# Logits in two parts, v in two buffers, eight plain heads, and constants moved to ScalarE and GpSimd

## The chip, the cores and the metric

The kernel runs on one core of a Trainium2 chip. The metric is the device time of one execution in microseconds (us). The core's engines work side by side, each through its own queue in program order: TensorE (PE, with its weight loads as PEld), VectorE (DVE), ScalarE (ACT), GpSimd (POOL) and SyncE (SP), which only issues DMAs. An instruction waits for semaphores of the engines or DMAs that make its operands or free its output.

## What is computed

Attention over 4 batches of 12 heads, then a mixture of experts in which each token goes to one of 8.

```python
scores = scale * np.matmul(q, k.transpose(0, 1, 3, 2))       # (4, 12, 448, 64) each
scores = np.where(mask, -1000000000.0, scores)
attn = np.exp(scores - np.max(scores, axis=-1, keepdims=True))
attn = attn / (np.sum(attn, axis=-1, keepdims=True) + 1e-09)
x = np.matmul(attn, v)                                        # to (1792, 768)
logits = x @ w_gate + modality_bias[modality_id]              # (1792, 8)
e_idx = np.argmax(logits, axis=1)
gate_w = softmax(logits)[np.arange(N), e_idx]
for e in range(E):
    mask = e_idx == e
    h = np.maximum(x[mask] @ w1[e], 0.0)
    out[mask] = gate_w[mask, None] * (h @ w2[e])
```

## The kernel before

**Attention** is a software pipeline over 48 heads, `iteration(n)` for n = 0 to 47. Iteration n makes the scores of head n on PE (`st_scores`, L270) and their masked maximum on DVE (L280), the exponentials of head n-1 on ACT (`st_exp`, L290), the transposes of head n-2 on PE (`st_trans`, L302), its split into a high and a low part on ACT (`ph`, L320) and DVE (`pl`, L321), and the product with v of head n-3 (`st_pv`, L334 and L341, into the one PSUM bank `ot`). The output of head n-4 is put together on ACT (`hol`, L359) and DVE (`ut`, L365), which frees `ot`. Four heads are a group. `st_comb` (L394) multiplies a group's outputs, one of four row tiles in each iteration, by a matrix that holds the gate weights, into the one PSUM bank `x`, eight iterations behind the scores. `norm_l` (L412) and `norm_x` (L422) divide by the softmax sums; row tiles 0 to 2 do so on DVE straight from `x`, tile 3 is copied to `cxt` by ACT and divided on POOL. `rec`, the sums plus 1e-9 (`st_sums`, L372, on POOL), is inverted on DVE.

**Operands.** Each product is three float32r products of a high and a low part; six heads, 0 to 5, use plain float32 operands, four matmuls in place of eight shorter ones. The parts of q and k are made on POOL one pair of heads ahead of use (`split_qk`, L194 and L195, and `split_kl`, L200 and L202, four iterations ahead of the pair) and stacked by four DMAs on SP. The parts of v are made on POOL once in a group (`split_vh`, L242, and `split_vl`, L247, in iterations 2, 6, 10 and so on) from one buffer `vraw`.

**Routing.** `after_batch` sets the routing of a batch into the iterations that follow it, in lists of work that `run_todo` takes up at fixed places of an iteration. The gate logits of three groups lie in the tile `ltp`; `logits` (L454, DVE) sums them, `top`, `ties` and `choice` find the expert (DVE and POOL; `oh` is the choice as 0 and 1), and `places` counts with small matmuls into bank `x` (L476 to L482) at which place of its expert's list a token stands. ACT copies the counts to `pc` (L485). `scatter` writes tokens into four tables in DRAM by indirect DMAs (L501). After batch 1 `first_expert`, `first_slot`, `first_shift`, `first_base`, `first_tri` and `first_order` choose the expert that is computed first and set constants of the schedule, on DVE (L516 to L537) and POOL.

**Between attention and experts** the last heads and batch 3 are worked off, written out by hand: `w1_chunk` splits the first expert's weights on POOL, `pre_g1` does first-layer products (L751 to L753) of two blocks of tokens that are known already, six steps of 6 matmuls for each block. In between stand the choice and `places` of batch 3. `schedule_a` is one long chain of small DVE instructions (L580 to L589) on the final counts; `htl` (L782, DVE) is the low part of the hidden layer, which the second-layer products need. After it come the expert blocks, whose token lists are fetched from the tables (L720) and gathered (L732).

## Time and profile before

| | us |
|---|---|
| median of 3 runs | 498.74 (497.79 to 500.5) |
| the profiled execution | 498.88 |
| its span in the trace | 496.8 |
| PE busy | 470.7 (95%) |
| DVE, ACT, POOL busy | 290.3, 276.4, 245.8 |
| mean granted clock of TensorE | 0.987 |

The span runs from the first to the last instruction; some 2.1 us of the profiled time lie outside it. Attention takes the first 209 us or so, the experts the rest. The shares of busy time are means over both: in attention all four engines are busy nearly all the time, among the experts PE alone is. A waiting engine appears as a gap, with the instruction whose end released it. The granted clock is 1.00 at 2.4 GHz and 0.50 at 1.2 GHz.

### The profile page before, as it was taken

To read this page: it belongs to the slowest core of one execution; us is meant where nothing else is said; L and a number is where in the kernel's file an instruction comes from. 1 tells how busy PE (TensorE), PEld (TensorE's weight loads), DVE (VectorE), ACT (ScalarE), POOL (GpSimd) and SP (SyncE) were. 2 spreads that over 40 slices of the span, in tenths; PEclk is the share of its full clock that TensorE was granted. 3 is DMA by queue.
4 is the path that set the end of the run, shared out by engine and by line. 5 is a ranking of instruction groups with operands and counts; after the bars stand their busy time and mean duration, and the time that the engine had idled before them with its cause. 6 is when DMAs were issued, how large, how long until landed. Compare 5 with 4: busy or idle time off the path is not lost. (4 is left out here: it accounts for less than half of the span.)

```text
span 496.8 us, 10248 instructions
## 1 busy us (share of the span) xinstructions
PE 470.7 (95%) x3307; PEld 443.0 (89%) x3307; DVE 290.3 (58%) x858; ACT 276.4 (56%) x680; POOL 245.8 (49%) x332
## 2 busy tenths in 40 slices
PE   8999899999899979989999999999999999999990
PEld 6799899999798979869999999999999999889770
DVE  4899899999889988987422017431120120283490
ACT  5799899999788978326212116612220211383670
POOL 8999999999999999942301104102001001021131
PEclk9999999999899999989999999999999999999997
DMA  7797799998987889491596204853001001076200
GB/s 189 199 257 214 183 236 251 281 237 206 292 214 182 188 182 327 126 202 3 163 381 208 81 1 144 292 203 98 34 1 53 33 2 63 33 279 194 104 13 7
DMA packets 43816, 78.91 MB, mean 159 GB/s; under 512 B 15582, under 2 KB 27614, under 8 KB 43744
## 3 DMA queue, kind: packets, MB, share of 16 engines
q1 hardware_dynamic: 40624, 66.94, 49.2%
q0 software_dynamic: 3040, 11.03, 6.6%
q8 instruction: 28, 0.46, 0.5%
q14 instruction: 44, 0.36, 0.3%
q10 hardware_dynamic: 80, 0.11, 0.1%
HBM read 48.10 MB, written 11.89 MB: 121 GB/s over the span
## 5 line engine op out<-in xcount | busy, mean ns | idle before, releaser
L732 POOL DMA_INDIRECT xg<-xs,idg x18 | 21.0, 1164 | 156.6 <-DVEq L1336 80.8
L290 ACT ACTIVATE p<-p,nm 128x448 f32<-128x448 f32 x192 | 94.8, 498 | 2.5 <-DVE nm L280 2.5
L770 DVE SCALAR_TENSOR_TENSOR htl<-g,hth 128x256 fp32r<-128x256 f32 x40 | 16.7, 425 | 104.6 <-ACT hth L769 104.6
L751 PE MATMUL g<-xh,w1h 128*128 128x256 f32 x240 | 67.1, 280 | 0.4 <-DVE htl L770 0.4
L753 PE MATMUL g<-xh,w1l 128*128 128x256 f32 x240 | 67.3, 280 | 0.0
L752 PE MATMUL g<-xl,w1h 128*128 128x256 f32 x240 | 67.0, 279 | 0.0
L321 DVE TENSOR_TENSOR pl<-pt,ph 128x1024 fp32r<-128x1024 f32 x48 | 58.3, 1215 | 7.6 <-ACT ph L320 7.2
L302 PE MATMUL pt<-ident,p 128*128 128x128 f32 x480 | 60.2, 273 | 0.0
L302 PEld LDWEIGHTS pt<-ident,p 128*128 128x128 f32 x480 | 55.3, 141 | 1.1
L334 PE MATMUL ot<-ph,vhl 128*128 128x448 f32 x192 | 50.5, 303 | 5.9 <-DVE ut L365 5.9
L320 ACT ACTIVATE ph<-pt 128x1024 fp32r<-128x1024 f32 x48 | 49.1, 1023 | 7.4 <-PE pt L302 6.3
L769 ACT ACTIVATE hth<-g 128x256 fp32r<-128x256 f32 x40 | 15.1, 383 | 63.5 <-PE g L753 63.5
L751 PEld LDWEIGHTS g<-xh,w1h 128*128 128x128 f32 x240 | 44.9, 187 | 0.6 <-DVE htl L770 0.6
L811 POOL DMA_INDIRECT out_dram<-row,idg x14 | 16.2, 1157 | 59.1 <-ACTq L1320 33.5
L752 PEld LDWEIGHTS g<-xl,w1h 128*128 128x128 f32 x240 | 45.2, 188 | 0.0
L753 PEld LDWEIGHTS g<-xh,w1l 128*128 128x128 f32 x240 | 45.1, 188 | 0.0
L334 PEld LDWEIGHTS ot<-ph,vhl 128*128 128x128 f32 x192 | 33.2, 192 | 7.9 <-DVE ut L365 6.4
L280 DVE CUSTOM_DVE_ANT_0 p<-sa,mask 128x448 f32<-128x448 f32 x96 | 36.2, 412 | 5.2 <-PE sa L270 4.9
L290 ACT ACTIVATION_READ_ACCUMULATOR p<-p,nm 128x1 f32 x192 | 36.5, 190 | 0.0
L280 DVE CUSTOM_DVE_ANT_0 p<-sb,mask 128x192 f32<-128x192 f32 x96 | 36.3, 411 | 0.0
L341 PE MATMUL ot<-pl,vhl 128*64 128x64 f32 x192 | 35.1, 298 | 0.7 <-DVE pl L321 0.7
L359 ACT ACTIVATE hol<-ot 64x448 f32<-64x448 f32 x48 | 26.0, 542 | 13.3 <-PE ot L334 10.8
(365 smaller groups left out, 1307.6 us busy)
## 6 DMA issues: line engine op xcount, KB each, us to landing
st<-hl SPq DMA_DIRECT2D x56, 224.0 KB
raw<-in_moe_w_dram SPq DMA_DIRECT2D x24, 512.0 KB
raw<-in_qk_dram SPq DMA_DIRECT2D x21, 448.0 KB
raw<-in_moe_w_dram SPq DMA_DIRECT2D x20, 384.0 KB
vraw<-in_v_dram SPq DMA_DIRECT2D x12, 384.0 KB
xs<-row SPq DMA_DIRECT2D x9, 384.0 KB
w1h<-hl SPq DMA_DIRECT2D x14, 224.0 KB
w1l<-hl SPq DMA_DIRECT2D x14, 224.0 KB
```

What stands on the lines that cost most here:

```text
L280: V.tensor_tensor_reduce(out=z, in0=o, in1=m, scale=-scale, scalar=3.0e38, op0=ALU.add, op1=ALU.min, accum_out=nm[:n, i:i + 1],)
L290: A.activation(out=z, in_=z, func=AF.Exp, bias=nm[:n, i:i + 1], scale=-1.0, accum_out=sums[:n, b, i, h:h + 1],)
L302: nc.tensor.transpose(out=o, in_=a, identity=i)
L320: A.activation(out=ph, in_=t, func=AF.Copy)
L321: V.tensor_tensor(out=pl, in0=t, in1=ph.bitcast(F32), op=ALU.subtract)
L334: nc.tensor.matmul(o[:, q0:S], lhsT=t[:rows, kt, h].rearrange("p a d -> p (a d)"), rhs=ph[:rows, c0:c1], start=(n == 0), stop=(n == 1),)
L341: nc.tensor.matmul(o[0:D, q0:S], lhsT=t[:rows, kt, h, 0], rhs=pl[:rows, c0:c1], start=False, stop=False)
L359: A.activation(out=t, in_=ov[g][64:128, :S], func=AF.Copy)
L732: P.indirect_dma_start(out=xg[u][:n], out_offset=None, in_=xs[0:rows, :], in_offset=bass.IndirectOffsetOnAxis(ap=g[:n, 0:1], axis=0), boun ...
L751: nc.tensor.matmul(o, lhsT=ah, rhs=bh, start=first, stop=False)
L752: nc.tensor.matmul(o, lhsT=ah, rhs=bl, start=False, stop=False)
L753: nc.tensor.matmul(o, lhsT=al, rhs=bh, start=False, stop=last)
```

## The change

- Heads 6 and 7 are plain as well (`first_load(3)`): their splits on POOL and stacking DMAs fall away, and DVE fills two half tiles with zeros.
- v has a second buffer, `raw1[2]`. The high part is made in iterations 7, 11, 15 and so on, the low part an iteration later; the first group's low part is made on DVE.
- `st_sums` is an ACT instruction.
- `part_logits` sums the first two groups' logits and the bias in iteration 19, 31 and 43; `logits` adds the third group's an iteration later. For batch 3 both stand in a row.
- `first_counts` reads the counts of batch 1 from bank `x` itself, right behind `places` and the split of head 33. The other constants go from DVE to POOL, the last ten instructions behind attention.
- Constants of the tables are made in iterations 1 and 3 (4 and 6 to 11 before), and the tables' clearing is issued in iteration 1 (4 before). Table rows stand 64 bytes apart (8 before), so that the tables grow from 14592 to 20480 rows.
- For the weights of the first expert, `w1_chunk` 0 to 2 stand in iterations 46, 47 and 47 in place of 45 to 47.
- 12 of the `pre_g1` matmuls go ahead of the `places` of batch 3, and `w2_chunk(2)` goes behind a transposition. 32 warming matmuls stand ahead of the first scores, 24 before.

The diff, cut to its core:

```diff
-    EMPTY = E * NT
-    NROW = EMPTY + 2 * BLK
+    STEP = 8
+    SHIFT = 64
+    EMPTY = STEP * (NT + E * SHIFT)
+    NROW = EMPTY + STEP * 2 * BLK
...
+    vraws = [vraw, raw1[2].rearrange("p (t c) -> p t c", t=NTL)]
+    def v_of(gr):
+        return vraws[gr > 1 and gr % 2 == 0]
...
-    def st_sums(gr, eng):
+    def st_sums(gr):
...
-        eng.tensor_scalar(
-            out=r.rearrange("p t h o -> p t (h o)"), in0=sums[:, b, :, u * GH:(u + 1) * GH],
-            scalar1=1.0, scalar2=1e-9, op0=ALU.mult, op1=ALU.add,
+        A.activation(
+            out=r.rearrange("p t h o -> p t (h o)"), in_=sums[:, b, :, u * GH:(u + 1) * GH],
+            func=AF.Copy, bias=1e-9,
...
+    def part_logits(b):
+        t = lts[b % 2]
+        V.tensor_reduce(
+            out=t[:, :, R0 + 1, :], in_=t[:, :, 0:R0 + 1, :].rearrange("p t h e -> p t e h"), axis=AX, op=ALU.add
+        )
...
-            V.tensor_reduce(out=lg, in_=lt_all.pop(b).rearrange("p t h e -> p t e h"), axis=AX, op=ALU.add)
+            V.tensor_reduce(
+                out=lg, in_=lt_all.pop(b)[:, :, R0 + 1:, :].rearrange("p t h e -> p t e h"), axis=AX, op=ALU.add
+            )
...
+    def first_counts():
+        fe["cnt"] = cnt = sm([128, E], "cnt")
+        fe["m"] = m = sm([128, 1], "fm")
+        V.tensor_tensor(out=cnt, in0=fe.pop("pos")[:, NP:NP + E], in1=ebase, op=ALU.subtract)
+        V.tensor_reduce(out=m, in_=cnt, axis=AX, op=ALU.max)
...
     def first_shift():
-        V.tensor_scalar(out=shift, in0=fe["m"], scalar1=float(2 * BLK), scalar2=None, op0=ALU.is_lt)
-        V.scalar_tensor_tensor(out=now, in0=by_shift[1], scalar=shift, in1=by_shift[0], op0=ALU.mult, op1=ALU.add)
+        P.tensor_scalar(out=oh0, in0=fe["t"], scalar1=xf, scalar2=0.0, op0=ALU.is_equal, op1=ALU.add)
+        P.tensor_scalar(out=shift, in0=fe["m"], scalar1=float(2 * BLK), scalar2=0.0, op0=ALU.is_lt, op1=ALU.add)
+        P.tensor_scalar(out=now, in0=by_shift[1], scalar1=shift, scalar2=0.0, op0=ALU.mult, op1=ALU.add)
+        P.tensor_tensor(out=now, in0=now, in1=by_shift[0], op=ALU.add)
...
-        for _ in range(24):
+        for _ in range(32):
             nc.tensor.matmul(warm_bank[:, 0:128], lhsT=ones, rhs=ones, start=True, stop=True)
...
+                todo[n + 4, 1] = [first_counts]
                 later(n + 6, first_expert)
-                before(n + 7, first_slot)
-                for j, f in enumerate((first_shift, first_base, first_tri, first_order)):
-                    later(n + 9 + j, f)
+                before(n + 8, first_max)
+                later(n + 8, first_slot)
...
                 st_split(n - 2)
+                run_todo((n, 1))
             if 0 <= n - 3 < NHEAD:
                 st_pv(n - 3)
...
-            if n % GH == 2 and n // GH + 1 < B * NG:
+            if n == 1:
+                split_vl(0, V)
+            if n == 2 or n % GH == 3 and n > GH and n // GH + 1 < B * NG:
                 split_vh(n // GH + 1)
-                split_vl(n // GH + 1)
+            if n == 2 or n % GH == 0 and n > GH:
+                split_vl((n + 2) // GH, P)
...
         w1_chunk(5, P)
+        for f in (first_shift, first_base, first_tri, first_order):
+            f()
         st_pv(n - 2)
...
+        part_logits(B - 1)
         for i in range(NTL):
             norm_l(g, i)
...
         pre_g1(0, (3, 4))
+        pre_g1(0, (5,))
+        pre_g1(1, (0,))
         places()
-        pre_g1(1, (0, 1, 2, 3))
+        pre_g1(1, (1, 2, 3))
```

Three places of the order that this gives. In the rows the operand written stands ahead of the arrow, and a wait names the engine (or DMA queue) that is waited for.

PE in iteration 35, before: from the end of the `places` of batch 1 to the scores of head 35's successor.

```order
L482 MATMUL x<-oh,ones 128x8
L334 MATMUL ot<-ph,vhl 128x448 [waits DVE_49]
L334 MATMUL ot<-ph,vhl 128x192
L341 MATMUL ot<-pl,vhl 64x64
L341 MATMUL ot<-pl,vhl 64x448
L334 MATMUL ot<-ph,vhl 128x64
L341 MATMUL ot<-pl,vhl 64x192
L341 MATMUL ot<-pl,vhl 64x320
L334 MATMUL ot<-ph,vhl 128x320
L394 MATMUL x<-wi,ut_133 128x144 [waits Activation_49]
L394 MATMUL x<-wi,ut_133 128x144
L270 MATMUL sa<-w1h_149 128x448 [waits DMAHW4_49,DMAHW3_49,DVE_49]
```

PE at the same place after:

```order
L503 MATMUL x<-oh,ones 128x8
L346 MATMUL ot<-ph,vhl 128x448 [waits DVE_49]
L346 MATMUL ot<-ph,vhl 128x192
L353 MATMUL ot<-pl,vhl 64x64
L353 MATMUL ot<-pl,vhl 64x448
L346 MATMUL ot<-ph,vhl 128x64
L353 MATMUL ot<-pl,vhl 64x192
L353 MATMUL ot<-pl,vhl 64x320
L346 MATMUL ot<-ph,vhl 128x320
L406 MATMUL x<-wi,ut_132 128x144 [waits DVE_49,Activation_49]
L406 MATMUL x<-wi,ut_132 128x144
L282 MATMUL sa<-w1h_148 128x448 [waits DMAHW2_49,DMAHW1_49]
```

The matmuls are the same; the one of `st_comb` (L406, before L394) now waits for DVE too. What it waits for stands in DVE's order at the same place, before:

```order
L379 RECIPROCAL rec<-rec 128x16 [waits Pool_49]
L321 TENSOR_TENSOR pl<-pt,ph 128x1024 [waits PE_49,Activation_49]
L365 TENSOR_TENSOR ut_132<-ot,hol_135 64x448 [waits Activation_49]
L412 TENSOR_TENSOR ltp<-x,rec 64x32 [waits DVE_49,PE_49]
L422 TENSOR_TENSOR xr<-x,rec 64x256
```

and after:

```order
L391 RECIPROCAL rec<-rec 128x16
L333 TENSOR_TENSOR pl<-pt,ph 128x1024 [waits PE_49,Activation_49]
L548 TENSOR_TENSOR cnt<-x,ebase 128x8 [waits PE_49]
L549 TENSOR_REDUCE fm<-cnt 128x1 [waits DVE_49]
L377 TENSOR_TENSOR ut_131<-ot,hol_134 64x448 [waits Activation_49]
L425 TENSOR_TENSOR ltp<-x,rec 64x32 [waits PE_49]
```

Two DVE instructions, of which the first reads bank `x`, now stand behind the split `pl` of head 33 and ahead of `ut`.

POOL at the end of batch 2, around the split of v for the last group and the division of row tile 3, before:

```order
L194 TENSOR_SCALAR hl<-raw_120 128x896 [waits DMAHW6_49,DMAHW5_49,DMAHW7_49,DMAHW4_49,DMAHW3_49]
L195 TENSOR_TENSOR hl<-raw_120,hl 128x448 [waits Pool_49]
L242 TENSOR_SCALAR vhl<-vraw 128x16x64 [waits DMAHW1_49,DMAHW0_49,PE_49]
L247 TENSOR_TENSOR vhl<-vraw,vhl 128x16x64 [waits Pool_49]
L412 TENSOR_TENSOR ltp<-cxt,rec 128x32 [waits Activation_49]
L422 TENSOR_TENSOR xr<-cxt,rec 128x256
L565 TENSOR_TENSOR tri_105<-tri_105,oh_95 128x64
L566 TENSOR_TENSOR tri_105<-tri_105,n_96 128x64 [waits Pool_49]
```

POOL at the same place after:

```order
L254 TENSOR_SCALAR vhl<-raw_117 128x16x64 [waits DMAHW7_49,DMAHW6_49,PE_49]
L196 TENSOR_SCALAR hl<-raw_120 128x896 [waits DMAHW6_49,DMAHW5_49,DMAHW7_49,DMAHW4_49,DMAHW0_49]
L197 TENSOR_TENSOR hl<-raw_120,hl 128x448 [waits Pool_49]
L259 TENSOR_TENSOR vhl<-raw_117,vhl 128x16x64
L202 TENSOR_TENSOR xl<-raw_120,hl 128x448 [waits PE_49]
L204 TENSOR_SCALAR qz_153<-raw_120,half 128x448 x2
L196 TENSOR_SCALAR hl<-raw_118 128x896 [waits DMAHW6_49,DMAHW5_49,DMAHW7_49,DMAHW4_49,DMAHW1_49]
L197 TENSOR_TENSOR hl<-raw_118,hl 128x448 [waits Pool_49]
L425 TENSOR_TENSOR ltp<-cxt,rec 128x32 [waits DVE_49,Activation_49]
L435 TENSOR_TENSOR xr<-cxt,rec 128x256
```

The low part of v no longer stands directly in front of the division (`ltp` and `xr` from `cxt`), and the two constants behind it are gone.

POOL at the end of attention, before: the last `w1_chunk`, the last division from `cxt`, and the first table.

```order
L675 TENSOR_SCALAR w1h_3199<-raw_121 128x1024 [waits DMAHW5_49]
L676 TENSOR_TENSOR w1l_3200<-raw_121,w1h_3199 128x1024 [waits Pool_49]
L412 TENSOR_TENSOR ltp<-cxt,rec 128x32 [waits Activation_49]
L422 TENSOR_TENSOR row<-cxt,rec 128x256
L501 DMA table_70<-ent,si 14592x2 [waits DMAHW2_49,DMASW4_49,DVE_49]
```

POOL at the same place after:

```order
L565 TENSOR_SCALAR oh_95<-ft,xf 128x8
L566 TENSOR_SCALAR shift<-fm 128x1
L567 TENSOR_SCALAR now<-by_shift_99,shift 128x4 [waits Pool_49]
L568 TENSOR_TENSOR now<-now,by_shift_98 128x4 [waits Pool_49]
L571 TENSOR_SCALAR eboff<-ebneg,now 128x8 [waits Pool_49]
L572 TENSOR_SCALAR eb_101<-ebneg,now 128x8
L592 TENSOR_SCALAR n_96<-oh_95 128x8
L593 TENSOR_TENSOR ctri<-ctri,n_96 128x64 [waits Pool_49]
L596 TENSOR_TENSOR ctri<-ctri,oh_95 128x64 [waits Pool_49]
L597 TENSOR_TENSOR ctri<-ctri,n_96 128x64 [waits Pool_49]
L425 TENSOR_TENSOR ltp<-cxt,rec 128x32 [waits Activation_49]
L435 TENSOR_TENSOR row<-cxt,rec 128x256
```

Ten small instructions now stand between the last `w1_chunk` (L706 and L707, ahead of these rows) and that division.

## Rows read from the trace of the kernel before

**Rows 1.** The page: granted clock in 40 slices of 12.4 us (9: full).

```profile
PEclk9999999999899999989999999999999999999997
```

**Rows 2.** What PE waited for: line, releaser, us in total, times, longest.

```profile
PE ot L334 <- DVE ut L365: 5.9, 6, 2.1
PE x L476 <- DVE row L422: 1.6, 1, 1.6
PE sa L270 <- POOL qz L202: 1.6, 1, 1.6
...
PE x L480 <- POOL oh L470: 0.4, 1, 0.4
```

**Rows 3.** Four heads, 60 to 75 us: length, busy of PE, PEld, DVE, ACT, POOL, clock.

```profile
60.44:75.04 14.60, 14.60 (x124) 14.33 (x122) 14.09 (x48) 14.41 (x42) 14.18 (x17) 1.00 1.01 229
```

**Rows 4.** Stretches, L270 on PE alone: length, busy (x instructions, eight per head), clock.

```profile
54.93:64.07 9.14, 2.91 (x16) 1.00 0.74 200
82.36:90.47 8.11, 2.70 (x17) 1.00 1.04 306
123.96:138.87 14.91, 4.47 (x25) 0.89 1.00 282
150.44:159.47 9.03, 2.92 (x16) 1.00 0.80 206
170.60:188.69 18.09, 5.26 (x33) 1.00 0.82 205
17.35:21.48 4.13, 2.05 (x8) 1.00 0.80 231
25.41:28.64 3.23, 1.30 (x8) 1.00 0.99 269
```

**Rows 5.** POOL alone, a stretch of attention and the sum over all of it.

```profile
100.00:120.00 20.00, 19.04 (x22) 1.00 0.92 219
...
sum 209.80, POOL 196.83; mean POOL 65.61
```

**Rows 6.** Timeline at the end of batch 1: start, us, engine, line, [idle before, releaser].

```profile
126.55 2.40 POOL L247 TENSOR_TENSOR vhl<-vraw,vhl 128x1024 fp32r<-128x1024 f32 x1
...
129.18 0.93 DVE L454 TENSOR_REDUCE lg<-ltp 128x32 f32<-128x416 f32 x1 [1.58 <-POOL ltp L412]
...
132.16 0.74 PE L334 MATMUL ot<-ph,vhl 128*128 128x448 f32 x2 [2.11 <-DVE ut L365]
```

**Rows 7.** Timeline, iteration 35: PE and DVE behind the places of batch 1.

```profile
142.77 0.65 PE L394 MATMUL x<-wi,ut 128*128 128x144 f32 x4
...
143.15 1.23 DVE L321 TENSOR_TENSOR pl<-pt,ph 128x1024 fp32r<-128x1024 f32 x1 [0.87 <-ACT ph L320]
```

**Rows 8.** Timeline, PE: the warming matmuls.

```profile
1.12 2.74 PE L892 MATMUL x<-ones 128*128 128x128 bf16 x24 [1.12 <-DVE warm L894]
```

**Rows 9.** Timeline, PE around the last choice, up to the second layer.

```profile
210.97 0.39 PE L752 MATMUL sb<-w1l,xh 128*128 128x512 f32 x1
211.21 0.40 PE L753 MATMUL sb<-w1h,xl 128*128 128x512 f32 x1
213.21 0.38 PE L476 MATMUL x<-pc,onesf 1*128 1x40 f32 x2 [1.61 <-DVE row L422]
...
225.89 0.42 PE L751 MATMUL ot<-w2h,hth 128*128 128x384 f32 x1
```

**Rows 10.** Timeline, DVE there: behind the places, the schedule's end, the low part.

```profile
214.07 0.19 DVE L490 TENSOR_TENSOR sl<-pc,oh 128x32 f32<-128x32 f32 x1 [0.68 <-issue]
...
223.19 0.15 DVE L583 TENSOR_SCALAR sch<-rr 128x1 int32<-128x1 f32 x1
...
224.96 0.69 DVE L782 TENSOR_TENSOR htl<-g,hth 128x512 fp32r<-128x512 f32 x1 [0.15 <-ACT hth L781]
```

**Rows 11.** Groups by line and shape: x count | busy us, mean ns | idle before.

```profile
L372 POOL TENSOR_SCALAR rec<-sums 128x16 f32<-128x16 f32 x11 | 2.2, 204 | 0.9
...
L485 ACT ACTIVATE pc<-x 128x40 f32<-128x40 f32 x4 | 0.8, 204 | 8.1 <-PE x L482 8.1
```

More of the change, by code (lines that the diff above doesn't have):

```diff
@@ L56, in attention_moe @@
     RECAT = 3
+    R0 = (NG - 1) * GH
     HB = BLK // 2
@@ L388, in st_comb @@
                 P.tensor_scalar(
-                    out=lts[b % 2][:, :, H, :], in0=mb[:, b], scalar1=1.0, scalar2=0.0, op0=ALU.mult, op1=ALU.add
+                    out=lts[b % 2][:, :, R0, :], in0=mb[:, b], scalar1=1.0, scalar2=0.0, op0=ALU.mult, op1=ALU.add
                 )
@@ L412, in norm_l @@
         eng.tensor_tensor(
-            out=lt_all[b][:n, i, u * GH:(u + 1) * GH, :], in0=xv[:, :, D:XW],
+            out=lt_all[b][:n, i, r:r + GH, :], in0=xv[:, :, D:XW],
             in1=rec[gr][:n, i].to_broadcast([n, GH, E]), op=ALU.mult,
@@ L484, in places @@
                 )
-            A.activation(out=pc, in_=pos[:, 0:NP + E], func=AF.Copy)
+            A.activation(out=pc, in_=pos[:, 0:NP + E], func=AF.Copy, scale=float(STEP))
             A.activation(out=pe[:, :, 0:E], in_=lg, func=AF.Exp)
             rt[b] = (pc, si)
+            fe["pos"] = pos
         def slots():
@@ L507, in route @@
         if b == B - 2:
-            choose = ((1, logits), (1, top), (1, ties), (2, first_tie), (-3, choice))
+            choose = ((1, logits), (1, top), (1, ties), (2, first_tie), (2, choice))
         return choose, places, (slots, ranks), scatter
@@ L625, in schedule_a @@
         red(r, base)
-        ts(sch[:, 0:1], r, float(EMPTY), 0.0, ALU.add, ALU.add)
+        ts(sch[:, 0:1], r, float(EMPTY // STEP), float(STEP), ALU.add, ALU.mult)
         return seg, oh
@@ L713, in fetch_ids @@
             if t == 0 or PZ <= t < SZ:
[L714 removed]
+                src = tables[i][bass.ds(off, BLK, STEP), :]
             elif t < PZ:
                 o = d[:, i]
[L717 removed]
+                src = tables[i][bass.ds(off, 2 * BLK, STEP), :].rearrange("(b p) c -> p b c", p=BLK)
             else:
[L719 removed]
+                src = tables[i][bass.ds(off, HB, STEP), :].rearrange("(o p) c -> o p c", o=1).to_broadcast([2, HB, 2])
             nc.sync.dma_start(out=o, in_=src)
@@ L917, in attention_moe @@
             eng.memset(praw[s][3][:, 448:512], 0.0)
+        for a in range(2):
+            V.memset(first_view(3, a)[64 - a * 64:128 - a * 64], 0.0)
         wg = w_gate.rearrange("(j a p) e -> a p j e", a=2, p=64)
@@ L966, in attention_moe @@
         for j in range(2):
-            later(3 + j, lambda j=j: V.memset(xg[j], 0.0))
+            later(2 * j, lambda j=j: V.memset(xg[j], 0.0))
             later(1 + j, lambda j=j: V.memset(sls[j][64:128, 0, E:E + 1], 1.0e6))
@@ L991, in setup_1 @@
             P.tensor_copy(e8v, e8)
-            fma(ebase, evals[:, 0, :], float(NT), 0.0)
-            fma(ebneg, ebase, 1.0, -float(EMPTY))
+            fma(ebase, evals[:, 0, :], SHIFT + 1.0 / STEP, 0.0)
+            fma(ebneg, ebase, 1.0, -float(EMPTY // STEP))
+            fe["eb"] = sm([128, E], "cnt")
+            fma(fe["eb"], ebase, float(STEP), 0.0)
         later(0, setup_0)
         later(1, setup_1)
-        later(2, lambda: V.memset(e8v[64:128, 0], 0.0))
+        later(3, lambda: V.memset(e8v[64:128, 0], 0.0))
         def setup_4():
@@ L1001, in setup_4 @@
             P.iota(ent[:, :, 1:NTL, 0], pattern=[[S, B], [128, NTL - 1]], base=64, channel_multiplier=1)
-            for i in range(NTL):
-                nc.sync.dma_start(out=tables[i].rearrange("(p r) c -> p r c", p=128), in_=fill)
             it = row()
@@ L1034, in after_batch @@
             choose, places, rank, scatter = st
+            later(n, lambda: part_logits(b))
             for j, f in choose:
                 later(n + j, f) if j > 0 else before(n - j, f)
-            last = b == B - 2
+            if b == B - 2:
+                before(n + 3, lambda: w1_chunk(0, P))
+                before(n + 4, lambda: w1_chunk(1, P))
+                later(n + 4, lambda: w1_chunk(2, P))
             soon(n + 4, places)
@@ L1073, in open_psm, with clear_tables @@
             mo["ps"] = ctx.enter_context(tc.tile_pool(name="psm", bufs=4, space=PSUM, reuse_waits="tile"))
-        for k in range(KA):
-            later(NHEAD - KA + k, lambda k=k: w1_chunk(k, P))
-        later(4, setup_4)
+        def clear_tables():
+            for i in range(NTL):
+                nc.sync.dma_start(out=tables[i].rearrange("(p r) c -> p r c", p=128), in_=fill)
+        later(1, setup_4)
         for s in range(2):
             for j in range(3):
-                later(6 + 3 * s + j, lambda s=s, j=j: shift_slots(s, j))
+                later(3, lambda s=s, j=j: shift_slots(s, j))
         def iteration(n):
-            if n % 2 == 1 and 5 < n + 3 < NHEAD:
+            if n % 2 == 1 and 7 < n + 3 < NHEAD:
                 stack_qk((n + 3) // 2)
-            if n == 1:
-                load_v(1)
-            if n and n % GH == 0 and n // GH + 1 < B * NG:
-                load_v(n // GH + 1)
             gr, i = divmod(n - 2 * GH, GH)
@@ L1267, in attention_moe @@
             x_store(B - 1, i)
-        pre_g1(0, (5,))
         ha, hb = (relu(o, i) for i, o in enumerate(g1b[0]))
-        w2_chunk(2)
         pre_g1(1, (4,))
@@ L1273, in attention_moe @@
         h_trans(0, ha, 0, pa)
+        w2_chunk(2)
         w2_chunk(3)
```

81 lines of the change are left out of this document (45 added, 36 removed).

## Prediction

> **What bounds the kernel now.** I first asked what PE waits for, since it is busy 95% of the span. The table of its waits [rows 2] is short: six waits on `ut` of DVE (5.9 us together), one of 1.6 us on POOL's `qz`, one of 1.6 us ahead of the last places, and smaller ones. So at most some 15 us can be had from waits, and a little from the clock, which dips in two slices of the page [rows 1], the 11th (from 124 us) and the 18th (from 211 us).
>
> Then I looked at an undisturbed stretch [rows 3]. Four heads take 14.60 us, 3.65 a head; PE is busy for all of it, and ACT (14.41), POOL (14.18) and DVE (14.09) nearly so. A saved instruction on one of the others brings nothing there; only disturbed stretches can give time. A disturbed stretch costs its length less 3.65 us per head [rows 4]: two heads around 57 us 9.14 - 7.30 = 1.84 (POOL's `qz` was late); the end of batch 0 8.11 - 7.30 = 0.81; that of batch 1 14.91 - 10.95 = 3.96; two heads around 154 us, where DVE makes the first expert's constants, 9.03 - 7.30 = 1.73; the end of batch 2, four heads, 18.09 - 14.60 = 3.49. Together 11.8 us.
>
> Why the batch ends stall is seen in the timeline [rows 6]. DVE's sum of the logits waits 1.58 us for POOL's division of the last row tile, which stands behind the low part of v (2.40 us). DVE is then late with `ut`, and PE waits 2.11 us. The clock follows: of the 3.96 us, 2.1 are the wait, and about 1.8 the half clock (1.2 in place of 2.4 GHz) that PE had behind it. So a fall costs 1.8 us here. POOL is late because it is never idle: 196.8 of the first 209.8 us are busy [rows 5], the rest mostly gaps between its instructions.
>
> **The change part by part**, against the profiled execution of 498.88 us (span 496.8, 2.1 outside it; the median is 0.14 less, so the sum holds for it as well).
>
> *POOL is relieved.* Heads 6 and 7 no longer need a split and four stacking DMAs, v's first low part goes to DVE, and eleven sums (204 ns each [rows 11]) go to ACT. Two pairs' splits and v's two parts fill nearly all of POOL's 14.18 us per four heads [rows 3]; less v's low part of 2.40 [rows 6] that is under 5.9 a pair, and I take 4.5. With v's first low part at 2.4 and the sums at 2.2, about 9 us go, against some 2 us of small constants that POOL takes over (ten at 0.2 [rows 11]). PE waited only 1.6 us at 57 us [rows 2], and two thirds of what goes lies before that. I take all 1.84 us there as gained. Moreover v's low part now stands behind the division, not ahead of it; so DVE's sum of the logits finds its input.
>
> *Batch ends.* The sum is in two parts, 9 rows of logits an iteration earlier (where DVE has no division) and 5 rows at the old place. By its 0.93 us for 13 rows, the first costs about 0.65 and the second about 0.40 us (estimates by size), so some 0.5 us go off the place that sets `ut`. I leave 0.3 us of delay at each end: batch 0 gives 0.5, batch 1 3.7 with its clock, batch 2 3.2. The latter holds two waits on stacking DMAs, which come sooner when POOL splits sooner. The choice of batch 2 no longer waits behind a weight split: 0.4 [rows 2]. Sum of the gains so far, with the 1.7 of the next part: 1.8 + 0.5 + 3.7 + 1.7 + 3.2 + 0.4 = 11.3.
>
> *First expert.* The constants that DVE made around 154 us go to POOL or behind attention: 1.7 gained. In their place two small instructions read the counts from bank `x`, in iteration 35, and this makes **a new wait on PE**. The bank has one buffer. In the trace `st_comb` wrote it again at 142.77 [rows 7], as only ACT's copy had to be done. Now DVE must have read it, and on DVE that read stands behind `pl`, which starts at 143.15 when ACT is done with `ph`, and takes 1.23. So bank `x` is free at 144.38 plus about 0.2 for one small read, 144.6: PE stands 1.9 us, with the scores of head 36 queued behind. DVE cannot come sooner than `ph`, so 1.6 us is the lower end (the read at nothing); the upper is 2.5, with the read as long as DVE's sum of the logits, 0.93 [rows 6]. Cost: +1.9.
>
> *Two more plain heads.* Scores of a plain head take 2.05 us, of a split one 1.30 [rows 4]: 0.75 twice, +1.5, on the busiest engine, with nothing to hide it; if the early heads wait for something anyway it is down to 0.7. *Warming.* Eight more matmuls of 2.74/24 = 0.11 us [rows 8] would be +0.9, but PE waits there for DVE's memsets and for loads; 0 and 0.9 bound it, I take +0.4.
>
> *ScalarE's sums.* 0.2 us per group, by the nearest row of a small ACT instruction [rows 11], on an engine with 0.19 us left in four heads [rows 3]. Its busy time contains overlaps, so I take nothing, and 0.1 per group, 1.1 in all, as the upper end. Beside it, the Trainium skill (ScalarE: Activation LUTs, Rules for kernel authors) tells one to put an add on VectorE and not on ScalarE, since DVE is up to about three times as fast per element in bf16; here POOL's row and ACT's are both 204 ns, so the row speaks against the rule at this size.
>
> *The last choice.* Before, PE ends its matmuls at about 211.4, waits for the choice and starts the places at 213.21; behind them it has work until the second layer at 225.89 [rows 9]. The change puts 12 matmuls, 0.24 us apart [rows 9], 2.8 us, ahead of the places. That looks like the 1.6 us of waiting and the 1.8 us of half clock behind it (the page's second dip [rows 1]) gained, 3.4. But it shortens what lies between places and second layer, and DVE has a chain there: from 214.07 through the whole schedule to 223.19, then the low part `htl` at 224.96, 0.69 long, done at 225.65, 0.24 ahead of PE's need [rows 10]. It was just hidden. After: places at 211.4 + 2.8 = 214.2, 1.0 later; the schedule ends at 223.34 + 1.0 = 224.3; `htl` now comes straight behind (`w2_chunk(2)` has moved), done at 225.0; second layer about 225.2. That is 0.7 sooner, not 3.4. PE's work from 213.66 to 225.89 was 12.2; less 1.8 for the clock and 2.8 moved, 7.6 are left, done at 214.7 + 7.6 = 222.3. So PE waits nearly 3 us there, a wait longer than the two (2.1 and 1.6 plus the tiny places matmuls) that brought the clock down: +1.8 for a fall. Net +1.1. POOL's ten constants ahead of the last division, about 10 x 0.25 = 2.5 us, delay the choice, but the 2.8 us of matmuls cover that.
>
> *The rest* (tables' spacing, earlier setup, expert blocks): those transfers are far ahead of use, and I take nothing.
>
> **Sum:** 498.88 - 11.3 + 1.9 + 1.5 + 0.4 - 0.7 + 1.8 = 492.5. The fall of the clock in iteration 35 is left out: 1.9 us lies between a wait of 1.6 us that had none (around 57 us, the fifth slice [rows 1]) and the 2.1 us that had one; it is nearly even.
>
> **Rivals.**
> - *Both new waits bring the clock down*: 494.3. For it: the 213.21 wait of 1.6 had a fall. Chance 0.22.
> - *Neither does*, 490.7, or the DVE chain is shorter than I think and the last choice gives its whole 3.4: 491.4 - 3.4 = 488.0. Against the latter: each of its instructions waits for the one before. Together 0.25.
> - *The change does only half of what it says*: once POOL is in time, DVE (14.09 of 14.60) or ACT (14.41) cannot catch up after a batch end and PE waits almost as before; half of the 11.3 comes: 492.5 + 5.6 = 498.1. Chance 0.10.
> - *ACT becomes the bound*: the small sum takes three times its row, 0.6 us, and ACT overruns four heads by 0.4, eleven times: 492.5 + 4.5 = 497.0. Its row speaks against it. Chance 0.02. The rule on ScalarE named above is what would make it so.
> - *Slower: POOL stays late.* Its place is the batch ends, its condition that POOL is still some 7 us behind there. It is then behind for the qz stall as well: 1.8 + 0.5 + 3.7 + 3.2 + 0.4 = 9.6 us of gains fall away, the ten constants no longer fit under the 2.8 us of matmuls (about +0.8), and the new wait stays: 492.5 + 9.6 + 0.8 = 502.9, 501.1 without a further fall. Against it: POOL needs 14.18 less about 0.9 in four heads of 14.60 [rows 3], so it catches up. The Trainium skill (GPSIMD Engine Reference, Elementwise — side-by-side cycle accounting) has GpSimd 1.96 times slower than the Vector engine on an addition and keeps elementwise work off it, which speaks for this rival. Chance 0.08.
>
> **How the numbers follow.** The forecast of 492.5 has 0.33. Between 487.5 and 497.0 lie it, both clock rivals and part of the halved case: about 0.8. Some 0.5% (2.5 us) is what a measurement of this kernel tells from no change. Faster than 496.4: 0.33 + 0.22 + 0.25 and a little, 0.81. Within 0.5%: 0.11. Slower: 0.08.
>
> **What would show it.** In the trace of after: no wait on `qz` near 55 us; waits on `ut` at the batch ends under 0.5 us and no dip of the clock there; a PE wait near 2 us on DVE in front of `st_comb` of iteration 35; places of batch 3 without a wait, but a new wait of 2 to 3 us on `htl` in front of the second layer, with a dip behind. I am wrong if POOL is still without idle time up to the end of attention, if `st_comb` doesn't wait there, or if PE runs through to the second layer.

## The result and the profile after

| | before | after |
|---|---|---|
| median (range) | 498.74 us (496.83 to 500.5, 5 runs) | 493.61 us (492.11 to 494.63, 5 runs) |
| the profiled execution | 498.88 | 492.11 |
| its span | 496.8 | 490.2 |
| PE busy | 470.7 (95%) | 469.8 (96%) |
| DVE, ACT, POOL busy | 290.3, 276.4, 245.8 | 291.9, 277.2, 239.6 |
| mean granted clock | 0.987 | 0.989 |

The changed kernel takes 0.9897 of the time before (95% interval 0.986 to 0.9935). It is 1.0% faster, where the forecast of 492.5 meant 1.3%. The median lies 1.1 us above the forecast; the profiled execution, the shortest of the five, lies 0.4 us below it (492.11), so the two traces show 1.6 us more gain than the medians. That the sum came so near is in part luck: the start was put 2.3 us too dear, and the gains ahead of head 46 and at the last choice came out smaller by as much together. The lines of the code stand 2 to 31 lower now (L270 is L282, L334 is L346, L394 is L406, L476 is L497, L782 is L813).

The page's clock row of after, to be read against [rows 1]: the dip in the 11th slice is gone, the one in the 18th is there.

```profile
PEclk9999999999999999989999999999999999999997
```

What PE waited for, after: line, releaser, us in total, times, longest.

```profile
PE x L497 <- DVE row L435: 2.8, 1, 2.8
PE x L406 <- DVE cnt L548: 1.7, 1, 1.7
PE ot L346 <- DVE ut L377: 1.5, 4, 0.7
PE x L923 <- DVE warm L925: 1.1, 1, 1.1
PE ot L784 <- DVE htl L813: 0.7, 1, 0.7
```

Against [rows 2], the waits on `ut` fell from 5.9 to 1.5 us and the one on `qz` is gone. Two stand in their place: 2.8 us ahead of the last places (1.6 before), and 1.7 us at L406 (`st_comb`), which did not exist.

**Iteration 35**, the timeline of after (start, us, engine, line, [idle before, releaser]), the place of [rows 7]:

```profile
137.36 1.23 DVE L333 TENSOR_TENSOR pl<-pt,ph 128x1024 fp32r<-128x1024 f32 x1 [0.59 <-ACT ph L332]
...
138.50 0.15 DVE L548 TENSOR_TENSOR cnt<-x,ebase 128x8 f32<-128x8 f32 x1
...
138.80 0.73 PE L406 MATMUL x<-wi,ut 128*128 128x144 f32 x4 [1.66 <-DVE cnt L548]
```

DVE's `pl` waits for ACT's `ph`; the read of bank `x` stands behind `pl`; the matmul that writes `x` again waits for the read. Against before, head 36 loses 1.91 us on head 35. The clock stays at 1.00 behind this wait.

**The last choice**, POOL, DVE and PE in the timeline of after, the place of [rows 9, 10]:

```profile
198.68 2.36 POOL L707 TENSOR_TENSOR w1l<-raw,w1h 128x1024 fp32r<-128x1024 f32 x1
201.03 1.02 POOL L565 TENSOR_SCALAR oh<-ft,xf 128x8 f32<-128x8 f32 x1
...
204.61 0.30 POOL L597 TENSOR_TENSOR ctri<-ctri,n 128x64 f32<-128x64 f32 x1
204.87 0.24 POOL L425 TENSOR_TENSOR ltp<-cxt,rec 128x32 f32<-128x32 f32 x1
...
205.14 0.76 DVE L456 TENSOR_REDUCE ltp<-ltp 128x32 f32<-128x288 f32 x1 [3.12 <-POOL ltp L425]
...
208.16 0.18 DVE L491 TENSOR_SCALAR oh<-eq 128x32 bf16<-128x32 f32 x1
208.25 0.41 DVE L435 TENSOR_TENSOR row<-x,rec 64x256 f32<-64x256 f32 x1
...
208.81 0.38 PE L497 MATMUL x<-pc,onesf 1*128 1x40 f32 x2 [2.78 <-DVE row L435]
...
219.16 0.15 DVE L614 TENSOR_SCALAR sch<-rr 128x1 int32<-128x1 f32 x1
219.23 0.68 DVE L813 TENSOR_TENSOR htl<-g,hth 128x512 fp32r<-128x512 f32 x1
219.96 0.44 PE L784 MATMUL ot<-w2h,htl 128*128 128x384 f32 x1 [0.68 <-DVE htl L813]
```

POOL's ten constants (L565 to L597) take from 201.03 to 204.87, 3.84 us (of these about 0.7 come with the weight split ahead of them, see e1). Only then comes the division that DVE has been standing for (3.12 us idle). DVE sums and chooses until `oh` at 208.16, and PE, with the 12 matmuls that were put ahead already done, stands 2.78 us. What released PE is not `oh` itself but `row`: it reads bank `x`, which the first matmul of the places overwrites, and it runs from 208.25 to 208.66, behind `oh`. So this wait too ends with a reader of bank `x`, 0.47 us after `oh` is done; it was so before the change (`row` until 213.06, PE at 213.21). The clock falls behind that wait, as PE's windows of after show (window, length, busy, clock, DMA share, GB/s):

```profile
206.00:208.81 2.81, 0.03 (x2) 1.00 0.40 159
208.81:210.00 1.19, 1.19 (x10) 1.00 0.19 40
210.00:211.00 1.00, 1.00 (x4) 0.51 1.02 163
211.00:212.00 1.00, 1.00 (x4) 0.50 0.89 326
212.00:213.00 1.00, 1.00 (x3) 0.50 0.96 338
213.00:214.00 1.00, 1.00 (x5) 0.79 0.92 356
```

Over the last four windows 0.49 + 0.50 + 0.50 + 0.21 = 1.7 us are lost to the clock.

**An undisturbed stretch**, to be read against [rows 3]: four heads in the windows of after (length, busy of PE, PEld, DVE, ACT, POOL, clock).

```profile
101.00:115.60 14.60, 14.60 (x123) 14.32 (x122) 14.14 (x48) 14.40 (x43) 14.01 (x15) 1.00 0.81 211
```

ACT has 14.40 us with its new instruction (14.41 before), so the sums cost nothing that shows there.

**POOL** alone over all of attention, to be read against [rows 5]:

```profile
0.00:205.70 205.70, 190.53 (x284) 1.00 0.85 226
```

It is busy for 93% of the time (94% before). The prediction named a POOL "still without idle time" as a sign that it is wrong; by the letter that sign nearly came, with its longest waits 1.56 us at 74 and 1.06 us at 59 us, and it was badly chosen. What changed is how late POOL is. From the end of ACT's copy `cxt` to the start of POOL's division, the timeline of before has 4.6 to 8.6 us in the first eleven groups and 2.9 in the last; that of after has 0.1 to 1.4 in the first six, 1.2 to 3.0 in the next four, 5.8 and then 8.0 in the last two.

### The profile page after: what moved, and what is told of

Read it like the earlier page. It is cut to its first block, busy times and chain, and to the rows that moved or that the text cites. A ratio compares the mean times of both kernels' runs of the same rounds, so it can differ in the third digit from the quotient of the medians.

```text
span 490.2 us, 10270 instructions
## 1 busy us (share of the span) xinstructions
PE 469.8 (96%) x3315; PEld 442.0 (90%) x3315; DVE 291.9 (60%) x860; ACT 277.2 (57%) x692; POOL 239.6 (49%) x325
## 4 chain that ended last, share of the span: by engine, by line
PE 59%; DVE 23%; ACT 5%; POOL 5%; issue 5%; DMA 1%; SPq 0%; DVEq 0%; POOLq 0%; ACTq 0%
PE g L784 7%; PE g L782 7%; PE g L783 7%; DVE p L292 6%; DVE pl L333 5%; PE pt L314 3%; DVE ut L377 3%; PE sa L282 2%; PE sb L282 2%; PE ot L784 2%; PE ot L783 2%; PE x L784 2%; PE x L783 2%; PE x L782 2%; PE ot L782 2%
## 5 line engine op out<-in xcount | busy, mean ns | idle before, releaser
L782 PE MATMUL g<-xh,w1h 128*128 128x256 f32 x240 | 67.1, 279 | 0.4 <-DVE htl L801 0.4
L346 PE MATMUL ot<-ph,vhl 128*128 128x448 f32 x192 | 50.0, 301 | 1.7 <-DVE ut L377 1.5
L782 PEld LDWEIGHTS g<-xh,w1h 128*128 128x128 f32 x240 | 44.9, 187 | 0.6 <-DVE htl L801 0.6
L346 PEld LDWEIGHTS ot<-ph,vhl 128*128 128x128 f32 x192 | 32.8, 190 | 3.6 <-DVE ut L377 1.9
L406 PE MATMUL x<-wi,ut 128*128 128x144 f32 x180 | 29.4, 286 | 1.7 <-DVE cnt L548 1.7
```

The costliest lines, as they stand in the source:

```text
L346: nc.tensor.matmul(o[:, q0:S], lhsT=t[:rows, kt, h].rearrange("p a d -> p (a d)"), rhs=ph[:rows, c0:c1], start=(n == 0), stop=(n == 1),)
L406: nc.tensor.matmul(x[:, j * 2 * XW:(j + 1) * 2 * XW], lhsT=ots(gr, j)[:, q0:q0 + 128], rhs=wi[:, u * (GH // 2) + j].rearrange("p a c -> p ...
L782: nc.tensor.matmul(o, lhsT=ah, rhs=bh, start=first, stop=False)
```

## Experiments

The starting point of each is the kernel after; `[rows]` are still those of before. Single runs of one kernel spread by 1 to 2 us either way, with some 3 to 5.5 us above the median (e2, e5, e8), and head 2 starts up to 1.4 us sooner or later from one kernel's profile to another's, so differences under 1.5 us are read from the traces only.

**The theory** after the result: POOL's ten constants make the last choice late; moved behind it, the wait of 2.78 us and the fall go. Rivals: DVE, not POOL, is late; or the schedule's chain takes all of it.

### e1: the ten constants behind the last division

```diff
         w1_chunk(5, P)
-        for f in (first_shift, first_base, first_tri, first_order):
-            f()
...
         st_norm(g - 1, 3)
+        for f in (first_shift, first_base, first_tri, first_order):
+            f()
```

> The changed kernel with one thing moved: the ten small POOL constants stand behind the last division from cxt, ahead of the table writes. Theory (POOL's constants hold up the choice of batch 3): DVE's first logits part no longer waits 3.1 us, the places of batch 3 no longer wait 2.8 us, and the fall of the clock at 210 to 213 us (1.7 us) is gone; but DVE's schedule chain then ends only 2.8 us sooner, so PE waits about 2 us on htl in front of the second layer. Span 490.2 - 2.8 = 487.4, up to 489.1 if the clock falls there. Rival (the chain is not the bound): the whole 2.8 + 1.7 comes, span 485.7. Rival (the constants don't matter, the choice is late by itself): span 490.2.

Measured: 491.18 us (488.98 to 493.3, 4 runs), ratio 0.9861 (0.9806 to 0.9917), span 487.2. Its waits on PE:

```profile
PE ot L784 <- DVE htl L813: 2.0, 1, 2.0
PE x L406 <- DVE cnt L548: 1.7, 1, 1.7
PE sa L282 <- DMA st<-hl: 1.4, 2, 0.8
```

No wait and no fall at the places any more (`oh` starts at 205.39 in place of 208.16), and 2.0 us on `htl`, where the prediction saw nearly 3, with the clock at 1.00 behind it. In this trace the theory held. The constants are worth less than their 3.84 us, as POOL's rows in e1 show:

```profile
201.29 0.95 POOL L425 TENSOR_TENSOR ltp<-cxt,rec 128x32 f32<-128x32 f32 x1
...
202.80 0.32 POOL L565 TENSOR_SCALAR oh<-ft,xf 128x8 f32<-128x8 f32 x1
```

Now the division stands behind the weight split and takes 0.95 us in place of 0.24, and L565 takes 0.32 in place of 1.02. The 0.7 us belong to the place behind the split, so the constants cost about 3.1.

The four executions of e1 took 488.98, 489.22, 493.14 and 493.3 us, at mean granted clocks of 0.991, 0.991, 0.988 and 0.988. The trace is of the one at 489.22, so it does not show where the other two lost 4 us; their mean clock is lower by 0.003, about 1.5 us of the time, near to what one fall costs (1.7 us in after).

### e2 and e3: the counts from ACT's copy, and both

```diff
-        V.tensor_tensor(out=cnt, in0=fe.pop("pos")[:, NP:NP + E], in1=ebase, op=ALU.subtract)
+        V.scalar_tensor_tensor(
+            out=cnt, in0=rt[1][0][:, NP:], scalar=1.0 / STEP, in1=ebase, op0=ALU.mult, op1=ALU.subtract
+        )
```

DVE reads the counts from `pc` in SBUF, so bank `x` is free as it was before the change. e3 has this and e1's edit.

> The changed kernel with the counts of batch 1 read from ACT's copy pc (divided by 8) in place of bank x, at the same place of DVE's order. Theory (one buffer of bank x makes PE wait for DVE): the wait of 1.7 us in front of st_comb in iteration 35 is gone, span 490.2 - 1.7 = 488.5. Rival (PE would wait on DVE or ACT there anyway, a few instructions later): span 490.2, with the wait moved to ut or to the next head.

> Both edits, the constants behind the last division and the counts from ACT's copy. Theory: the two gains add, span 490.2 - 1.7 - 2.8 = 485.7 if the clock holds in front of the second layer, 487.4 if it falls there. Rival (DVE and POOL are what bounds attention, so a PE wait taken away in iteration 35 comes back at the end): span as with the constants alone.

Measured: e2 493.14 us (492.37 to 496.87, 10 runs), 0.9915 (0.9888 to 0.9942), span 491.1; e3 493.04 (489.96 to 493.56, 4 runs), 0.9865 (0.9818 to 0.9913), span 491.6. The wait at L406 is gone, and nothing is gained. PE's waits and the row of head 46 in the timeline of e2:

```profile
PE sa L282 <- DMA st<-hl: 3.0, 1, 3.0
PE ot L786 <- DVE htl L815: 2.1, 1, 2.1
```

```profile
178.21 0.44 PE L282 MATMUL sa<-st 128*128 128x448 f32 x1 [2.98 <-DMA st<-hl]
```

Head 46's stacking DMAs now land 2.98 us (2.60 in e3) after PE wants them, and the clock is 0.50 from 180 to 182. SP issues a 512 KB load of the first expert's weights at 168.91 and the four stacking DMAs from 169.82 to 172.89, behind it; from 172 to 174 the DMA engines are at a share of 1.02. In after PE came to this head at 176.91 and found its operands there; in e2 it stood from 175.23 to 178.21. So 1.7 us of the new wait are PE's coming sooner, and at least 1.3 are DMAs that landed later than in after; why they did is open.

### e9 and e10: that weight load one iteration later

```diff
-        W1AT = (9, 11, 12, 13, 14, 15)
+        W1AT = (9, 12, 12, 13, 14, 15)
```

e9 is e1 with this edit, e10 is e3 with it.

> As with the constants later, and the second 512 KB load of the first expert's weights is issued behind the stacking DMAs of the last pair of heads, not ahead of them. Theory (bytes queued ahead of the stacking hold up head 46): its wait of 0.8 us is gone, span 487.2 - 0.8 = 486.4. Rival (POOL is late with the parts that are stacked): the wait stays, span 487.2.

> As with both edits (constants later, counts from ACT's copy), and the second weights load behind the stacking of the last pair. Theory (bytes queued ahead of the stacking gave the new wait of 2.6 us at head 46, and the clock fell behind it): 512 KB less at about 400 GB/s are 1.3 us, so the wait falls to 1.3 us or less and the clock holds: span 491.6 - 1.3 - 1.7 = 488.6, or 487 and less if all of the wait goes. Rival (POOL is late with the parts that are stacked): 491.6, the wait in iteration 35 has only moved.

Measured: e9 493.76 us (489.87 to 494.24, 6 runs), 0.9881 (0.9846 to 0.9916), span 488.0; e10 491.84 (490.85 to 493.42, 6 runs), 0.9856 (0.9824 to 0.9889), span 489.3. In e9 and in e10 head 46 waits for nothing (0.80 us in e1, 2.60 in e3), which shows that the load ahead of them had made the stacking DMAs late. In time e9 gains nothing: its median is that of after, with two executions at 489.87 and 490.89 us and four at 493.7 to 494.2. In e10 another fall took part of the gain, behind the wait of 1.93 us on `htl`. PE's windows there:

```profile
214.00:216.95 2.95, 1.02 (x8) 1.00 0.02 3
216.95:219.00 2.05, 2.05 (x9) 0.80 0.14 3
219.00:221.00 2.00, 2.00 (x8) 0.50 0.11 2
221.00:225.00 4.00, 4.00 (x25) 0.93 0.17 3
```

The same wait of 2.03 in e1, 2.17 in e9, 2.08 in e2 and 2.05 in e3 had none.

### e4 and e11: the 12 matmuls behind the places again

```diff
         pre_g1(0, (3, 4))
-        pre_g1(0, (5,))
-        pre_g1(1, (0,))
         places()
-        pre_g1(1, (1, 2, 3))
+        pre_g1(1, (0, 1, 2, 3))
...
+        pre_g1(0, (5,))
```

e4 is e3 with this edit, e11 is e9 with it.

> As with both edits, and the 12 first-layer matmuls stand behind the places of batch 3 again, as in the kernel before. Theory (what lies ahead of the places is taken from the cover of DVE's schedule chain): the places wait some 2 us for the choice and the clock falls behind them, but the second layer finds htl done: 0 to 1.7 us more than with both edits. Rival (the matmuls ahead of the places save their wait and the fall of the clock for good): 3.4 us or more above both edits.

> As with the constants and the weights load later, and the 12 first-layer matmuls behind the places of batch 3 again. Theory (what lies ahead of the places is taken from the cover of DVE's schedule chain): the places wait 2 us for the choice, the second layer no longer waits 2.0 us on htl; span as without this edit, up to 1.7 us more if the clock falls behind the places. Rival (the matmuls ahead of the places are a gain of their own): 2 to 3.4 us more.

Measured: e4 492.72 us (491.81 to 493.43, 4 runs), 0.9876 (0.9838 to 0.9914), span 491.1; e11 496.23 (493.67 to 498.71, 12 runs), 0.9942 (0.9919 to 0.9965), span 492.0. Against e3 the edit costs nothing; against e9 it costs 4.0 us of span (2.5 in the medians). The timelines of all these kernels, side by side, say why (us from the span's start):

| kernel | places | wait ahead of them | first matmul with `htl` | between | wait on `htl` |
|---|---|---|---|---|---|
| before | 213.21 | 1.61, fall | 226.33 | 13.12 | none |
| after | 208.81 | 2.78, fall | 219.96 | 11.15 | 0.68 |
| e1 | 206.25 | none | 217.27 | 11.02 | 2.03 |
| e3 | 209.95 | none | 220.95 | 11.00 | 2.05 |
| e4 | 209.58 | 0.90 | 221.14 | 11.56 | none |
| e9 | 206.24 | none | 217.40 | 11.16 | 2.17 |
| e10 | 206.05 | 0.30 | 216.95 | 10.90 | 1.93, fall |
| e11 | 205.48 | 2.58, fall | 221.24 | 15.76 | none |

With the 12 matmuls ahead, 10.9 to 11.2 us lie between, whatever PE does: that is DVE's chain through the schedule. With them behind, PE's own work takes 11.56 (e4), hardly more. So the reorder itself is worth about half a microsecond; what it can bring beyond that is that PE does not stand at the places and the clock does not fall there. In e11 it stood 2.58 us and then ran at half clock for more than 6 us:

```profile
202.90:205.48 2.58, 0.00 (x1) 0.98 0.78 237
205.48:207.00 1.52, 1.52 (x9) 0.50 0.91 350
...
211.00:212.00 1.00, 1.00 (x4) 0.50 0.39 131
212.00:213.00 1.00, 1.00 (x6) 0.90 0.02 3
```

In e4 PE was already late by its wait at head 46 and stood 0.90 us, without a fall. And in after, where the places waited 2.78 us, the fall behind it cost little of its own: the chain took 11.15 us all the same, and PE's wait on `htl` shrank from 2.0 to 0.68.

### e5 and e6: the two halves of the change at the batch ends

e5 sums all logits at the old place (the row for the first part is set to zero, so it adds 14 rows); e6 has v's parts in the old iterations, both on POOL.

```diff
e5
-                out=lg, in_=lt_all.pop(b)[:, :, R0 + 1:, :].rearrange("p t h e -> p t e h"), axis=AX, op=ALU.add
+                out=lg, in_=lt_all.pop(b).rearrange("p t h e -> p t e h"), axis=AX, op=ALU.add
...
-            later(n, lambda: part_logits(b))
e6
-            if n == 2 or n % GH == 3 and n > GH and n // GH + 1 < B * NG:
+            if n % GH == 2 and n // GH + 1 < B * NG:
                 split_vh(n // GH + 1)
-            if n == 2 or n % GH == 0 and n > GH:
-                split_vl((n + 2) // GH, P)
+                split_vl(n // GH + 1, P)
```

> The changed kernel with the logits summed in one part (14 rows, of which one is zero) where the second part stands. Theory (POOL being in time is what freed the batch ends, the two parts only shorten DVE's work there by some 0.5 us): the waits on ut at the three batch ends grow from 0.3 to about 0.8 us each, span 490.2 + 1.5 = 491.7; the end of batch 3 stays, as DVE waits there for POOL anyway. Rival (the two parts are what freed them): the waits return to 2.1 and 1.3 us with a fall of the clock, span 490.2 + 5 = 495.

> The changed kernel with v split as before, both parts in iterations 6, 10 and so on, ahead of the division of the fourth row tile; the two buffers and their loads stay. Theory (POOL's relief matters, not the order of v): in the trace of the changed kernel POOL divides 0.1 to 2.9 us behind ACT's copy, and DVE wants the result 4 us later at the ends of batches 0 and 1, so 3.4 us more fit there; at the end of batch 2 it is just even. Span 490.2 to 490.7. Rival (the order matters): DVE waits 1.5 us at the ends of batches 1 and 2, span 490.2 + 3 to 5 = 493 to 495.

Measured: e5 494.33 us (492.78 to 497.47, 10 runs), 0.9935 (0.9909 to 0.9961), span 491.3; e6 496.96 (494.56 to 499.17, 10 runs), 0.9983 (0.9956 to 1.0009), span 493.8. PE at the end of batch 1, in after and in e5:

```profile
127.90 0.47 PE L346 MATMUL ot<-ph,vhl 128*128 128x448 f32 x1 [0.28 <-DVE ut L377]
```

```profile
128.26 0.56 PE L346 MATMUL ot<-ph,vhl 128*128 128x448 f32 x2 [0.81 <-DVE ut L377]
```

At the place that sets `ut`, the second part of the sum takes 0.47 us and the whole sum 1.04 (L473 in after and e5), and PE waits 0.5 to 0.6 us less at each of the three ends. v's order moved nothing at the ends (0.25, 0.28 and 0.23 us in e6); my reason for it fell. It matters elsewhere: with v's parts in the old iterations one of POOL's pair splits comes late behind the indirect DMAs of a table, and e6 has a new wait there,

```profile
162.54 0.47 PE L282 MATMUL sa<-xh,w1h 128*128 128x448 f32 x1 [1.24 <-POOL w1h L204]
```

and POOL is later still at the last choice (places at 212.25 against 208.81).

### e7 and e8: six plain heads, and the sums on POOL

```diff
e7
-        first_load(3)
+        load_qk(3)
...
-            if n % 2 == 1 and 7 < n + 3 < NHEAD:
+            if n % 2 == 1 and 5 < n + 3 < NHEAD:
e8
-        A.activation(
-            out=r.rearrange("p t h o -> p t (h o)"), in_=sums[:, b, :, u * GH:(u + 1) * GH],
-            func=AF.Copy, bias=1e-9,
+        (V if gr == B * NG - 1 else P).tensor_scalar(
+            out=r.rearrange("p t h o -> p t (h o)"), in0=sums[:, b, :, u * GH:(u + 1) * GH],
+            scalar1=1.0, scalar2=1e-9, op0=ALU.mult, op1=ALU.add,
```

> The changed kernel with heads 6 and 7 split and stacked again. Theory (the plain heads cost PE 0.75 us each, and the relief that they give POOL is not needed, since POOL idles in the first 60 us): span 490.2 - 1.5 = 488.7. Rival (they are what removed the wait on qz at 57 us): that wait is back with up to 1.8 us, and POOL stays later at the batch ends: span 490.5 or more.

> The changed kernel with the sums plus 1e-9 on POOL (the last on DVE), as before. Theory (POOL is late again from batch 2 on, 8 us behind ACT's copy at the last division): eleven times 0.29 us come on top at the end, the choice of batch 3 is 1 to 3 us later, span 491 to 493. Rival (they are hidden on either engine): 490.2. Rival (ACT is the bound and is relieved): 488 to 489.

Measured: e7 497.03 us (494.37 to 498.96, 10 runs), 0.997 (0.9944 to 0.9997), span 494.2; e8 494.6 (493.97 to 500.11, 10 runs), 0.9941 (0.991 to 0.9971), span 492.3. e7's expectation, that six plain heads would be 1.5 us faster, fell: it is 4.0 us of span slower (3.4 in the medians). The wait on `qz` at 57 us, which the rival had back, did not return, but PE had lost 3.8 us against after by then; so e7 does not settle what removed it. PE's timeline in e7:

```profile
28.12 0.47 PE L282 MATMUL sa<-xh,w1h 128*128 128x448 f32 x1 [2.62 <-POOL w1h L204]
```

POOL is late there because 17 small constants stand ahead of the pair's split, 4.4 us in a row from 21.97, which in the trace of before are spread from 31 to 55 us. Fitting them there is what the two further plain heads pay for. e8 is as fast as after up to head 45, then waits 1.88 us on head 46's stacking DMA, with a fall: eleven instructions of 0.2 us on POOL cost 2.1 us of span where POOL is late at the end (1.0 in the medians). In after each sum took 203 ns on ACT, whose busy time in four undisturbed heads did not grow. The rule of the Trainium skill (ScalarE: Activation LUTs, Rules for kernel authors) puts an add on VectorE rather than ScalarE. No run here has all the sums on DVE; the one that stood there in before (L372) took 206 ns, so at this size the two engines cost about the same. (The prediction set POOL's row against ACT's, which says nothing of DVE.)

## Why the prediction came out

Its steps, against the starts of the heads in both timelines (after minus before). The measured column is of the profiled execution of after, the shortest of its five; small drifts between the steps make up the 0.07 us by which its rows miss their sum.

| step | predicted, us | measured, us |
|---|---|---|
| two more plain heads, warming, start: up to head 14 | +1.9 | -0.44 |
| the stall at 57 us | -1.8 | -1.87 |
| end of batch 0 | -0.5 | -0.12 |
| end of batch 1 with its clock | -3.7 | -3.32 |
| `st_comb` in iteration 35 | +1.9 | +1.91 |
| first expert | -1.7 | -1.75, then +0.4 behind it |
| end of batch 2, to head 46 | -3.2 | -2.9 |
| sum up to head 46 | -7.1 | -8.16 |
| from there to the first matmul with `htl` | +0.7 (-0.4 - 0.7 + 1.8) | +1.8 |

**Right, by their place and size:** the stall on `qz`, the first expert, the end of batch 1 with its dip of the clock, and, by its mechanism too, above all the new wait in iteration 35: the chain `ph`, `pl`, read of `x` costs what was worked out from [rows 7]; PE's wait is 1.66 us and the delay 1.91. That no fall came there was left open as nearly even. The waits on `ut` at the ends are 0.29, 0.28 and 0.29 us. But the stretches of [rows 4] are still 0.56, 0.64 and 0.86 us longer than undisturbed heads, where 0.3 was left, and so each end gave a little less than forecast. e5 shows that the sum in two parts makes 0.5 to 0.6 us of the gain at each end. That the rest is POOL's being in time agrees with its lateness in the two traces, but it is not shown which part of the relief did it: e6, e7 and e8 each take one part back (v's order, the plain heads, the sums), and in none does the wait of 2.1 us at the end of batch 1 or the wait on `qz` return. No run takes them all back, and none puts the first expert's constants back on DVE.

**Wrong, too dear:** the start. The plain heads and warming were put at +1.9. The heads themselves cost +0.6 (head 6's stretch +0.69, head 7's -0.12), near the lower end of 0.7; the first scores come 0.28 us later. But head 2 makes up 0.57 us, and PE's wait for the first `pl` (0.71 us before, in head 3's stretch) went away. Part of that is the run: over the experiments with eight plain heads, head 14 starts between 1.0 us sooner and 1.4 us later than before. What e7 adds was not in the prediction at all: with POOL's constants drawn forward, the plain heads are needed.

**Wrong, the step that failed:** the last choice. Two things were said: POOL's ten constants, 2.5 us, are covered by the 2.8 us of matmuls; and PE waits for `htl` with a fall of the clock, +1.8. The first fails by the prediction's own figures: PE stood 1.6 us at the places before, so only 1.2 of the 2.8 us were left to cover a later choice (213.2 + 2.5 = 215.7, with PE there at 214.2). Against that, POOL's last division was in time before, as these rows of before show: it was done at 209.18, and DVE's sum began at 210.19 without a wait.

```profile
208.23 0.95 POOL L412 TENSOR_TENSOR ltp<-cxt,rec 128x32 f32<-128x32 f32 x1
...
210.19 1.00 DVE L454 TENSOR_REDUCE lg<-ltp 128x32 f32<-128x416 f32 x1
```

Measured against the end of PE's matmuls, without the 12 that were moved (211.6 before, 206.0 - 2.8 = 203.2 after), this division ended 2.4 us ahead before and 1.9 us behind after. Of these 4.3 us the constants are about 3.1, not 2.5; the other 1.2 are what PE had gained on POOL by then. So PE stood 2.78 us at the places, which the prediction had without a wait. e1 takes the constants away and the whole wait and its fall with them, 3.0 us of span in the two traces. The rival "POOL stays late" had this in it, "the ten constants no longer fit under the 2.8 us", but tied to a POOL late at all batch ends, and priced at 0.8; POOL was nearly in time at the first two ends, and very late only at the last two divisions. The other half, the wait on `htl`, is real: with the constants gone it is 2.0 us (e1), and the 11.0 us that the prediction has between places and second layer (214.2 to 225.2) are the 10.9 to 11.2 of the table. (It took its 0.7 us from the first matmul of the second layer, at 225.89; the first that needs `htl` came at 226.33, so 1.1 would have been right.) But a wait there brought a fall in only one profile of five. So a term of +1.8 did not come, and a late choice, worth 2.7 us up to the first matmul with `htl`, came in its place. That these two and the start nearly cancel is luck.

The rival that "the last choice gives its whole 3.4" is refuted by the same table: with the 12 matmuls ahead, 11 us lie between wherever the places stand. "Both new waits bring the clock down" did not happen. "Neither does" did, by the letter: the clock held behind the 1.66 us in iteration 35 and behind the 0.68 us on `htl`; but it fell at the places, which that rival had without a wait. "Only half of what it says" fell with the 8.16 us that were there at head 46. "ACT becomes the bound" fell with ACT's 14.40 us. The rule that speaks against POOL, the Trainium skill's (GPSIMD Engine Reference, Elementwise — side-by-side cycle accounting), has an addition 1.96 times slower there than on the Vector engine. Rows here point the same way with a smaller ratio: the division of 128x32 logits (L425, a multiplication by the inverse) took 182 ns in the mean on DVE, and on POOL 232 to 250 ns in eleven cases of twelve; the twelfth, behind a weight split, took 1.22 us. What cost time was less that ratio than POOL's queue ahead of the division.

**Versions that go further:** e1 and e10 (491.18 and 491.84 us) are faster than before beyond doubt. They also lie some 2 us below after, but the intervals of the ratios overlap (0.9806 to 0.9917 and 0.9824 to 0.9889, against 0.986 to 0.9935); the traces bear it out up to the first matmul with `htl`, 2.7 and 3.0 us sooner than in after. As e9, which differs from e1 in one load only, has after's median, a gain over after in time is not shown. Open is what brings the fall behind the same wait on `htl` in one profile and not in another, and the 0.4 us lost around 158 us.

## What to carry to other kernels

When work is moved onto an engine that is late, its whole length falls on whatever stands behind it, and a cover is worth only what a wait on record has not used up already. Read at that place when the engine comes to the dependent instruction, not its mean load. A wait taken away is worth only what the next transfer or chain leaves of it (e2's 1.66 us and more went to a stacking DMA behind a 512 KB load), so look at what PE would meet if it came sooner. And where a second engine's chain sets the end, matmuls moved ahead of its start gained here only where a fall of the clock went with them.
